# Squared-ReLU attention into a GELU layer: value products copied out of PSUM whole, a first load in two transfers, an identity built on another engine

## The chip, the cores and the metric

The kernel runs on one core of a Trainium2 chip. A core has TensorE (PE; its weight loads are listed apart as PEld), VectorE (DVE), ScalarE (ACT), GpSimd (POOL) and SyncE (SP), each with its own instruction stream, and 16 DMA engines that all queues share. The metric is the device time of one execution in microseconds (us). The time before is 392.25 us, the median of 4 runs (392.04 to 392.69).

## The reference

Attention without softmax over 8 batches, 12 heads, 448 positions and a head size of 64, and then two matrix products with an exact GELU between them:

```python
scores = scale * np.matmul(q, k.transpose(0, 1, 3, 2))      # scale = 1/sqrt(64)
attn = np.maximum(scores, 0.0) ** 2 / S                      # S = 448
attn_out = np.matmul(attn, v)                                # 8, 12, 448, 64
x = attn_out.transpose(0, 2, 1, 3).reshape(B * S, H * D)     # 3584 x 768
h = x @ w_in                                                 # 768 x 2048
g = 0.5 * h * (1.0 + erf(h / sqrt(2)))
return g @ w_out                                             # 2048 x 768
```

All inputs and the output are float32; the kernel computes in bfloat16 with float32 sums.

## The kernel before

The twelve heads of a batch are worked as three *quads* of four heads. For each quad:

- q and k are brought into transposed form, qT and kT. For batches 0 and 1 TensorE transposes them against an identity matrix, `ident` (lines 437 and 465), and DVE or ACT copies the result out of PSUM (lines 308 and 310). From batch 2 on, DVE permutes them into pk and pq (lines 386 and 397) and SP issues DMA transposes (lines 489 and 498).
- TensorE computes scores into a PSUM tile `ps` (line 535), ACT or DVE takes the ReLU with the scale (lines 547 and 549) into `a_sq`, DVE squares it (line 556).
- When the seven blocks of a quad are squared, TensorE forms the value products (`add_av`, line 597) in a PSUM tile `pav` of two banks: 128 partitions x 2 x 448 columns (2 x 224 in batch 0, which is worked in two halves of the positions). Two copies, one for each bank, take them to `xT` in bfloat16 (lines 623 to 630). The planner puts each of the two on DVE or ACT.

The first matrix product (`psh`, line 644) reads a batch's whole xT and w_in, ACT takes the GELU into `h_sb` (line 656); the second (`pso`, line 687) reads h_sb and w_out, DVE copies it to `osb` (line 308) and SP stores it (line 710). The scores and value products of one batch are interleaved with the matrix products of the batch before.

PSUM has eight banks: three tiles of two banks in the pool `w` (ps and pav in turn) and two of one bank in the pool `f` (tp, psh, pso in turn). A tile is given out in turn, so a new ps waits until the tile given out three before it has been read.

The order of instructions on each engine is made when the program is built. The class `Scheduler` keeps, for each operation, its engines with their estimated costs, what it needs and what it frees; the text `ORDER` names the first 270 operations in the order in which they are issued, with the engine of each (P, A, D, G, S), and the rest is placed by the earliest start. So the instructions of all engines stand in one fixed order, and an engine never takes a later one first.

All casting loads go through POOL (lines 257, 274 to 276, 280, 341 and 359). At most eight of them are under way: a ninth is issued when the first has landed. From batch 3 on a load also stands behind `gate` on POOL (line 510), a small copy that reads the transposed q of the batch before, so that loads aren't moved while the transposes are. The k and q of the first quad go in float32 through the queues of ACT and SP instead (lines 771 and 772) and are cast by DVE and ACT: DVE takes the first four of the seven column groups of k (`K_CUT`), ACT q and then the other three. TensorE runs 45 small products of zeros (line 787) until these arrive.

Of the kernel before, what the change touches and what calls it, by code (L numbers as in the profile page):

```python
# [12 lines left out]
B, H, S, D = 8, 12, 448, 64  # L13
# [5 lines left out]
NK = S // KB  # L19
# [16 lines left out]
X_BIAS = -0.2  # L36
# [14 lines left out]
def cols(half):  # L51

    return slice(0, S) if half is None else slice(half * HS, half * HS + HS)
# [3 lines left out]
K_CUT = 4  # L57
# [1 line left out]


ORDER = """
G0 G1 G2 G3 G4 G5 A10 D13 G6 A16 P11 P14 G7 D12 A15 P17 G8 D18 P21 P39 D22 P33 P36 A34 D40
P19 D20 A37 P23 G9 P42 P48 D24 P54 A43 D35 A49 P51 D44 P25 D38 A52 D41 G117 A55 D53 P45 D50
A26 D47 A46 P57 D56 P69 P66 A58 D70 P27 G118 A67 P29 D59 P63 G119 A28 D71 P60 A64 G120 D68
P78 D61 A62 P75 A79 D65 P81 P31 D30 A76 D80 P96 G121 D32 A97 P72 D77 G122 A82 D98 P129 G123
D74 A73 P90 D130 P84 P108 A91 G124 D83 P131 A85 D109 P93 P141 D132 A94 D92 P102 D95 P105
P111 A103 D86 P143 D110 G125 A106 D104 P99 A112 D107 G126 A144 P87 D100 A101 D113 A142 P157
P114 D88 G127 A158 D89 P133 D115 A116 G128 P135 D159 A134 P160 P163 D136 P166 A164 P145 D167
A161 D165 P253 A146 D168 D162 P169 P172 G147 A254 P175 A173 D170 P245 G148 A176 D171 P255
A246 D177 G149 D174 P184 P187 A256 P196 A185 G150 D188 P137 P139 A138 P178 D197 G151 A140  # L70
D186 P193 P211 G152 D180 P247 A212 G153 D213 P249 A248 D179 A194 D198 G154 P263 A250 D195
D229 G155 P223 P220 A264 D189 P190 S235 A224 D221 P265 G156 A191 D225 P267 A266 D192 D222
P199 P217 A268 P214 D231 A218 P257 S236 D215 A200 D219 P259 A258 D216 D201 P181 P208 A260
P205 D230 A209 P261 D182 P251 D183 A262 D210 A206 D233 P202 A252 S237 D207 D232 P226 D234
A203 D204 S238 S239 P269
"""


class Op:
# [1 line left out]

    def __init__(self, engines, fn, deps=(), need=(), frees=(), bias=0.0, mode=None, joint=(),
                 other=0.0):
        self.engines, self.fn, self.deps = engines, fn, list(deps)
        self.need, self.frees, self.bias, self.mode = need, frees, bias, mode
        self.other = other
        self.joint = joint
        self.start = self.done = None  # L90


class Scheduler:
# [47 lines left out]
    def commit(self, est, op, eng, dur, lat):  # L141
        op.start = est
        if eng == "PE":
            self.mode = op.mode
            if est < self.COLD:
                dur, lat = 2 * dur, 2 * lat
        if isinstance(lat, tuple):
            t = max(self.dma, est + dur + 1.0)
            self.dma = t + lat[0] / 390e3
            op.done = self.dma + DMA_LAT  # L150
            self.landed += [op.done] * lat[1]
        else:
            op.done = est + lat
        self.free[eng] = est + dur
        for name in op.need:
            b = self.bufs[name]
            b[b.index(min(b))] = math.inf
        ends = [op.done] + [o.done for o in op.joint]
        if None not in ends:
            for name in op.frees:  # L160
                b = self.bufs[name]
                b[b.index(math.inf)] = max(ends)
        self.log.append((est, op, eng))

    def run(self, fixed):
# [40 lines left out]
def kernel(  # L206
# [9 lines left out]
    nc = tc.nc  # L216
# [24 lines left out]
    k32 = natpool.tile([128, 2, NK * D], F32, tag="pk", name="k32")  # L241
# [9 lines left out]
    def q_view(b, g0, g1, c0, c1):  # L251
        qq = q[b, 4 * g0 : 4 * g1].rearrange("h (p c) d -> p h (c d)", c=NC)
        return qq[:, :, c0 * D : c1 * D]
# [7 lines left out]
    def kv_view(t, b, g0, g1):  # L261

        return t[b, 4 * g0 : 4 * g1].rearrange("h s d -> (h s d)").rearrange(
            "(x p f) -> p x f", p=128, f=NK * D
        )
# [27 lines left out]
    ident = const.tile([128, 128], BF16, tag="ident", name="ident")  # L293
# [10 lines left out]
    V, A = nc.vector, nc.scalar  # L304

    def copy(eng, dst, src):
        if eng == "DVE":
            V.tensor_copy(dst, src)  # L308
        else:
            A.copy(dst, src)  # L310

    def e_copy(n, psum=4):

        d = 0.07 + n / psum / 960
        return ("DVE", d, d + 0.12), ("ACT", 0.12 + 0.00074 * n, 0.24 + 0.00074 * n)

    sch = Scheduler({"w": 3, "a": NA, "f": 2, "osb": 3})
# [10 lines left out]
    QK, SQ, AV, X, GL = {}, {}, {}, {}, {}  # L328
# [193 lines left out]
    def add_steps(todo, bias=0.0, dve=False):  # L522
        for blocks in todo:
# [55 lines left out]
            for blk in blocks:  # L579
                if blk[2] == NK - 1:  # L580
                    add_av(blk, bias)

    def add_av(blk, bias):
        b, g, _, half = blk
        blocks = [(b, g, i, half) for i in range(NK)]
        w = S if half is None else HS
        pav = []

        def fn(e_):
            pav.append(w_pp.tile([128, 2, NB], F32, tag="w", name="pav"))  # L590
            for i, x in enumerate(blocks):
                _, box, o = SQ[x]
                for j in range(2):
                    r = slice(64 * j, 64 * j + 64)
                    for e in range(2):
                        o2 = 64 * (e ^ j)
                        nc.tensor.matmul(  # L597
                            pav[0][o2 : o2 + 64, e, :w],
                            vt[b][r, 2 * g + e, bass.ts(i, D)],
                            box["a2"][r, e, o : o + w],  # L600
                            start=(i == 0),
                            stop=(i == NK - 1),
                        )

        deps = list(dict.fromkeys(SQ[x][0] for x in blocks)) + ld_v[b, g]

        last = {id(SQ[x][1]): x for x in SQ}
        gone = sum(last[id(SQ[x][1])] == x for x in blocks)
        d = 7 * 0.19 * w / S
        op = sch.add(  # L610
            (("PE", d, d + 0.24),), fn, deps, mode="A", bias=bias + AV_BIAS, need=("w",),
            frees=("a",) * gone,
        )
        AV[b, g, half] = op

        def get_x():
            if b not in xT:
                xT[b] = xpool.tile([128, HP, S], BF16, tag="xT", name="xT")
            return xT[b][:, 2 * g : 2 * g + 2, cols(half)]

        old = [o for (bb, *_), o in F1.items() if bb == b - 2]
        xs = X[b, g, half] = []
        for j in range(2):
            xs.append(
                sch.add(
                    e_copy(w, 1), lambda e, j=j: copy(e, get_x()[:, j], pav[0][:, j, :w]),
                    [op] + old, frees=("w",), joint=list(xs), bias=bias + X_BIAS,
                )
            )
        xs[0].joint = [xs[1]]  # L630


    def add_f1(b, m, half=None, bias=0.0):
# [96 lines left out]
    def f2(b):  # L730
        tiles = range(0, 3) if b % 2 == 0 else range(3, 7)
        return [(2.6, add_f2(b // 2, t, n)) for t in tiles for n in range(2)]

    def mix(a, b):

        a, b = list(a), list(b)
        r, n = [], len(a) + len(b)
        na = len(a)
        for i in range(n):
            if a and (not b or (na - len(a) + 1) * n <= (i + 1) * na):  # L740
                r.append(a.pop(0))
            else:
                r.append(b.pop(0))
        return r
# [12 lines left out]
    def slots(first, last):  # L757
# [10 lines left out]
        return out + [[("AV", done)]]  # L768


    nc.scalar.dma_start(k32, kv_view(k, 0, 0, 1))
    nc.sync.dma_start(q32, q_view(0, 0, 1, 0, HC))
    zero = const.tile([128, 128], BF16, tag="zero", name="zero")
    V.memset(zero, 0.0)  # L774
    V.memset(ident, 0.0)
    nc.gpsimd.affine_select(
        out=ident, in_=ident, compare_op=mybir.AluOpType.not_equal, fill=1.0,
        base=0, pattern=[[-1, 128]], channel_multiplier=1,
    )
    warm = const.tile([128, 1], F32, tag="warm", name="warm")  # L780
    V.memset(warm, 0.0)

# [22 lines left out]
    def early(eng, get, src, t):  # L805
        def fn(e):
            get_nat(0)
            copy(e, get(), src)

        n = src.shape[1] * src.shape[2]  # L810
        d = 0.07 + n / 960 if eng == "DVE" else 0.12 + 0.00074 * n
        return sch.add(((eng, d, d + 0.12),), fn, [landed(t)])

    o = early("ACT", lambda: nq[0][:, :4, : HC * D], q32, 5.3)
# [4 lines left out]
    for eng, i0, i1 in (("DVE", 0, K_CUT), ("ACT", K_CUT, NK)):  # L819
        c = slice(i0 * D, i1 * D)  # L820
        o = early(eng, lambda c=c: nk[0][:, :2, c], k32[:, :, c], 5.45)
# [42 lines left out]
    class at_slot:  # L864


        def __init__(self, n):
            self.key = first[n]
# [41 lines left out]
    x1, x2 = f1(B - 1), f2(B - 2)  # L910
    for _, o in x2[:1] + mix(x1, x2[1:]) + f2(B - 1):
        pe_q.append(o)
    sch.run({"PE": pe_q, "POOL": pool_q})
# [1 line left out]
_INS = ['q', 'k', 'v', 'moe_w_in', 'moe_w_out']  # L915
# [26 lines left out]
```

## Time and profile before

| | |
|---|---|
| Median of 4 runs | 392.25 us |
| The profiled execution | 392.41 us |
| Its span in the profile | 390.5 us |
| Granted TensorE clock | full in all 40 slices |
| PE, DVE, ACT, POOL busy | 98%, 49%, 51%, 12% of the span |
| Copies xT<-pav, 448 columns | 22 on DVE, mean 624 ns; 20 on ACT, mean 532 ns |
| Copies xT<-pav, 224 columns | 7 on DVE, mean 385 ns; 5 on ACT, mean 345 ns |
| First k, ACT's queue, 448 KB | 4.6 us from issue to landing |
| First q, SP's queue, 224 KB | 4.4 us from issue to landing |
| Affine select for ident, POOL | 311 ns, at 2.15 us |

A line of the timeline gives start, duration, engine, line of the code, operation, what is written from what, shapes, and in brackets how long the engine had been idle and what released it. PE is busy nearly throughout: its waits are few and have to be looked for one by one. A DMA's "landing" is the time at which those who wait for it may go on.

### The profile page before, as it was taken

To read this page: it belongs to the slowest core of one execution; us is meant where nothing else is said; L and a number is where in the kernel's file an instruction comes from. 1 tells how busy PE (TensorE), PEld (TensorE's weight loads), DVE (VectorE), ACT (ScalarE), POOL (GpSimd) and SP (SyncE) were. 2 spreads that over 40 slices of the span, in tenths; PEclk is the share of its full clock that TensorE was granted. 3 is DMA by queue.
4 is the path that set the end of the run, shared out by engine and by line. 5 is a ranking of instruction groups with operands and counts; after the bars stand their busy time and mean duration, and the time that the engine had idled before them with its cause. 6 is when DMAs were issued, how large, how long until landed. Compare 5 with 4: busy or idle time off the path is not lost.

```text
span 390.5 us, 7973 instructions
## 1 busy us (share of the span) xinstructions
PE 381.5 (98%) x3436; PEld 211.7 (54%) x3437; DVE 189.6 (49%) x350; ACT 200.1 (51%) x304; POOL 45.7 (12%) x69
## 2 busy tenths in 40 slices
PE   8799999998999999999999999999999999999996
PEld 7476554454555555555555555555555555555563
DVE  3999962466636435644555346545355352110121
ACT  4988855753436554565734466366536545222200
POOL 8665304000200200020000200000000000000000
PEclk9999999999999999999999999999999999999999
DMA  9999999999998691689139871370111011100132
GB/s 176 193 203 204 198 176 125 209 202 152 187 179 135 125 177 39 135 126 177 42 68 154 125 131 42 78 146 2 40 27 56 2 42 40 42 14 28 40 81 82
DMA packets 69523, 42.94 MB, mean 110 GB/s; under 512 B 37744, under 2 KB 65904, under 8 KB 69488
## 3 DMA queue, kind: packets, MB, share of 16 engines
q0 software_dynamic: 30512, 22.47, 38.5%
q1 hardware_dynamic: 38672, 19.49, 24.8%
q8 instruction: 27, 0.44, 0.4%
q10 hardware_dynamic: 304, 0.48, 0.3%
q14 instruction: 8, 0.07, 0.0%
HBM read 45.61 MB, written 11.01 MB: 145 GB/s over the span
## 4 chain that ended last, share of the span: by engine, by line
PE 85%; DMA 9%; POOL 2%; DVE 1%; SPq 1%; issue 1%; ACT 0%; POOLq 0%
PE pso L687 36%; PE psh L644 33%; PE ps L535 8%; PE pav L597 7%; DMA nq<-in_q_dram 5%; DMA nk<-in_k_dram 2%; DMA v_sb<-in_v_dram 2%; SPq L498 1%; DMA qT<-pq 1%; POOL nk L341 1%; DVE a_sq L556 0%; POOL nq L257 0%; POOL v_sb L359 0%; DVE osb L308 0%; DVE pq L397 0%
## 5 line engine op out<-in xcount | busy, mean ns | idle before, releaser
L644 PE MATMUL psh<-xT,win_sb 128*128 128x448 bf16 (+1 forms) x804 | 154.3, 345 | 0.1
L687 PE MATMUL pso<-wout_sb,h_sb 128*128 128x384 bf16 (+2 forms) x895 | 151.6, 326 | 0.1
L547 ACT ACTIVATE a_sq<-ps 128x896 bf16<-128x896 f32 (+1 forms) x141 | 123.3, 914 | 48.4 <-PE ps L535 48.2
L556 DVE TENSOR_TENSOR a_sq<-a_sq 128x896 bf16<-128x896 bf16 (+1 forms) x169 | 100.5, 618 | 53.7 <-ACT a_sq L547 53.5
L656 ACT ACTIVATE h_sb<-psh 128x448 bf16<-128x448 f32 x128 | 70.1, 547 | 98.5 <-PE psh L644 98.5
L687 PEld LDWEIGHTS <-h_sb 128*128 128x128 bf16 x896 | 86.2, 98 | 62.5 <-issue 5.8
L644 PEld LDWEIGHTS <-win_sb 128*128 128x128 bf16 x804 | 76.2, 98 | 70.4 <-issue 9.7
L308 DVE COPY osb<-pso 128x384 f32<-128x384 f32 (+2 forms) x56 | 31.2, 557 | 89.6 <-PE pso L687 89.6
L535 PE MATMUL ps<-qT,kT 64*64 64x448 bf16 (+1 forms) x756 | 46.8, 336 | 2.6 <-DVE a_sq L549 0.9
L549 DVE TENSOR_SCALAR a_sq<-ps 128x896 bf16<-128x896 f32 x28 | 30.4, 1090 | 36.0 <-PE ps L535 35.6
L597 PE MATMUL pav<-a_sq,v_sb 64*64 64x448 bf16 (+1 forms) x756 | 37.2, 330 | 0.9 <-ACT a_sq L547 0.4
L535 PEld LDWEIGHTS <-kT 64*64 64x64 bf16 x756 | 18.3, 105 | 24.3 <-issue 19.1
L597 PEld LDWEIGHTS <-v_sb 64*64 64x64 bf16 x756 | 21.3, 107 | 13.6 <-issue 2.7
L308 DVE CAST xT<-pav 128x448 bf16<-128x448 f32 (+1 forms) x29 | 16.3, 566 | 9.3 <-ACT xT L310 4.6
L310 ACT CAST xT<-pav 128x448 bf16<-128x448 f32 (+1 forms) x25 | 12.4, 495 | 15.4 <-PE pav L597 9.7
L510 POOL COPY gate<-qT 128x4 bf16<-128x4 bf16 x5 | 0.9, 188 | 157.3 <-DMA qT<-pq 157.3
L257 POOL DMA_DIRECT2D nq<-in_q_dram x14 | 11.6, 827 | 2.7 <-DMA win_sb<-in_moe_w_in_dram 0.9
L359 POOL DMA_DIRECT2D v_sb<-in_v_dram x14 | 10.6, 755 | 3.1 <-DMA win_sb<-in_moe_w_in_dram 1.9
L341 POOL DMA_DIRECT2D nk<-in_k_dram x13 | 10.0, 767 | 4.7 <-issue 1.5
L397 DVE COPY pq<-nq 112x512 bf16<-112x512 bf16 x36 | 8.2, 287 | 1.5 <-DMA nq<-in_q_dram 1.5
L386 DVE COPY pk<-nk 128x896 bf16<-128x896 bf16 x18 | 6.3, 386 | 1.0 <-DMA nk<-in_k_dram 1.0
L787 PE MATMUL spin<-zero 128*128 128x128 bf16 x45 | 5.0, 314 | 1.0 <-DVE zero L774 1.0
(26 smaller groups left out, 44.2 us busy)
## 6 DMA issues: line engine op xcount, KB each, us to landing
nk<-in_k_dram POOLq DMA_DIRECT2D x5, 672.0 KB, 7.7
nq<-in_q_dram POOLq DMA_DIRECT2D x5, 672.0 KB, 11.4
v_sb<-in_v_dram POOLq DMA_DIRECT2D x5, 672.0 KB, 13.8
out_dram<-osb SPq DMA_DIRECT2D x7, 336.0 KB, 2.8
wout_sb<-in_moe_w_out_dram POOLq DMA_DIRECT2D x2, 1152.0 KB, 11.7
out_dram<-osb SPq DMA_DIRECT2D x8, 288.0 KB, 2.8
v_sb<-in_v_dram POOLq DMA_DIRECT2D x9, 224.0 KB, 8.8
out_dram<-osb SPq DMA_DIRECT2D x8, 240.0 KB, 2.8
```

Of the source, the lines that this page charges most:

```text
L257: nc.gpsimd.dma_start(nq[b][:, 4 * g0 : 4 * g1, c0 * D : c1 * D], q_view(b, g0, g1, c0, c1))
L308: V.tensor_copy(dst, src)
L310: A.copy(dst, src)
L341: nc.gpsimd.dma_start(nk[b][:, 2 * g0 : 2 * g1], kv_view(k, b, g0, g1))
L535: nc.tensor.matmul(ps[64 * j : 64 * j + 64, e, x * w : x * w + w], kT[r, g, i * 128 + 64 * j : i * 128 + 64 * j + 64], qT[r, 2 * g + j, co ...
L547: A.activation(ar, ps, AF.Relu, scale=c_att)
L549: V.tensor_scalar(ar, ps, c_att, 0.0, op0=mybir.AluOpType.mult, op1=mybir.AluOpType.max,)
L556: V.tensor_mul(box["a2"][:, :, :used], ar, ar)
L597: nc.tensor.matmul(pav[0][o2 : o2 + 64, e, :w], vt[b][r, 2 * g + e, bass.ts(i, D)], box["a2"][r, e, o : o + w], start=(i == 0), stop=(i == ...
L644: nc.tensor.matmul(ph[:, x * n : x * n + n], win_sb[:, kd, bass.ts(m + x, 128)], xT[b][:, kd, c], start=(kd == 0), stop=(kd == KD - 1),)
L656: A.activation(hT[b // 2][:, m : m + nm, o + c.start : o + c.stop], box[0][:, :S].rearrange("p (x n) -> p x n", x=nm), AF.Gelu,)
L687: nc.tensor.matmul(po[:, :w], hT[pr][:, kf, bass.ts(t, 128)], wout_sb[:, kf, c], start=(kf == 0), stop=(kf == KF - 1),)
```

## The change

Three things are changed.

1. The value products of a quad leave PSUM in one copy of both banks on one engine, instead of two copies that may go to two engines. The operation's estimated cost is that of the whole size, and the tile is free when it is done, so the field `joint` (free when both are done) goes away.
2. The first k goes in two transfers of ACT's queue, one for each part of `K_CUT`, so that each cast waits for its own part.
3. The identity is an operation of its own on POOL, memset and affine select, at a place that ORDER names (`G1125`): behind the first three loads. Before, DVE cleared it, and POOL's affine select stood between the first load and the second.

ORDER is numbered anew, since there are fewer operations. In the changed program PE has the same instructions in the same order; DVE has 8 xT copies (4 of 2x224 and 4 of 2x448) and ACT 19 (2 of 2x224 and 17 of 2x448); where a merged copy stands between others on these engines differs from before in places.

```diff
-    def __init__(self, engines, fn, deps=(), need=(), frees=(), bias=0.0, mode=None, joint=(),
-                 other=0.0):
+    def __init__(self, engines, fn, deps=(), need=(), frees=(), bias=0.0, mode=None, other=0.0):
...
-        self.joint = joint
...
-        ends = [op.done] + [o.done for o in op.joint]
-        if None not in ends:
-            for name in op.frees:
-                b = self.bufs[name]
-                b[b.index(math.inf)] = max(ends)
+        for name in op.frees:
+            b = self.bufs[name]
+            b[b.index(math.inf)] = op.done
...
-        xs = X[b, g, half] = []
-        for j in range(2):
-            xs.append(
-                sch.add(
-                    e_copy(w, 1), lambda e, j=j: copy(e, get_x()[:, j], pav[0][:, j, :w]),
-                    [op] + old, frees=("w",), joint=list(xs), bias=bias + X_BIAS,
-                )
+
+        X[b, g, half] = [
+            sch.add(
+                e_copy(2 * w, 1), lambda e: copy(e, get_x(), pav[0][:, :, :w]),
+                [op] + old, frees=("w",), bias=bias + X_BIAS,
             )
-        xs[0].joint = [xs[1]]
+        ]
...
-    nc.scalar.dma_start(k32, kv_view(k, 0, 0, 1))
+    for i in (slice(0, K_CUT * D), slice(K_CUT * D, NK * D)):
+        nc.scalar.dma_start(k32[:, :, i], kv_view(k, 0, 0, 1)[:, :, i])
     nc.sync.dma_start(q32, q_view(0, 0, 1, 0, HC))
     zero = const.tile([128, 128], BF16, tag="zero", name="zero")
     V.memset(zero, 0.0)
-    V.memset(ident, 0.0)
-    nc.gpsimd.affine_select(
-        out=ident, in_=ident, compare_op=mybir.AluOpType.not_equal, fill=1.0,
-        base=0, pattern=[[-1, 128]], channel_multiplier=1,
-    )
...
+    def fn_ident(e):
+        nc.gpsimd.memset(ident, 0.0)
+        nc.gpsimd.affine_select(
+            out=ident, in_=ident, compare_op=mybir.AluOpType.not_equal, fill=1.0,
+            base=0, pattern=[[-1, 128]], channel_multiplier=1,
+        )
+
+    sch.add((("POOL", 0.4, 0.5),), fn_ident)
     sch.run({"PE": pe_q, "POOL": pool_q})
```

## The prediction

> **What bounds the kernel now.** I read the page first, for the engines' shares.
>
> ```profile
> PE 381.5 (98%) x3436; PEld 211.7 (54%) x3437; DVE 189.6 (49%) x350; ACT 200.1 (51%) x304; POOL 45.7 (12%) x69
> ```
>
> TensorE is busy 381.5 of 390.5 us, so 9.0 us is all that any change off TensorE can win. Of it 3.6 us is the tail (the last matmul ends at 386.9, then come a copy and the last stores). TensorE's waits are the rest; the trace lists them with total, times and longest:
>
> ```profile
> PE spin L787 <- DVE zero L774: 1.0, 1, 1.0
> PE ps L535 <- DVE a_sq L549: 0.9, 1, 0.9
> PE ps L535 <- ACT a_sq L547: 0.7, 2, 0.4
> PE tp L437 <- DMA nk<-in_k_dram: 0.5, 2, 0.4
> PE ps L535 <- ACT qT L310: 0.5, 1, 0.5
> ```
>
> Cut into windows, all of these but two fall before 20.7 us. TensorE then has no wait until 89, waits at 89.2 (0.15) and 90.7 (0.89), and never again. So the end is set by three things: when TensorE starts its unbroken run at 20.5, how long the stall at 89 to 91 is, and TensorE's own 296 us after it. The chain of waits and the timeline show what ends the two stalls:
>
> ```profile
> 13.35 7.11 DMA nk<-in_k_dram
> 66.51 19.27 DMA nq<-in_q_dram
> ```
> ```profile
> 20.50 0.58 PE L437 MATMUL tp<-ident,nk 128*64 128x128 bf16 x14 [0.19 <-DMA nk<-in_k_dram]
> 85.81 1.30 DVE L397 COPY pq<-nq 112x512 bf16<-112x512 bf16 x6 [1.52 <-DMA nq<-in_q_dram]
> 89.56 1.08 DVE L549 TENSOR_SCALAR a_sq<-ps 128x896 bf16<-128x896 f32 x1
> 90.70 0.38 PE L535 MATMUL ps<-qT,kT 64*64 64x448 bf16 x4 [0.89 <-DVE a_sq L549]
> ```
>
> Both hang on transfers: first keys of batch 1 land at 20.46; queries of batch 3 land at 85.78, VectorE then does six pq copies, an osb copy, three squares, an osb copy and a relu before a score tile comes free. In windows the DMA engines' share is 1.26 to 1.59 from 4 to 57 us at some 200 GB/s: POOL's queue always has a backlog, and a landing comes when the bytes ahead of it are through, not when it was issued.
>
> **Value products.** Before, a quad's two copies run one after the other: the second waits for the first.
>
> ```profile
> 134.83 0.53 ACT L310 CAST xT<-pav 128x448 bf16<-128x448 f32 x1 [0.49 <-PE pav L597]
> ...
> 135.40 0.62 DVE L308 CAST xT<-pav 128x448 bf16<-128x448 f32 x1 [0.27 <-ACT xT L310]
> ```
> ```profile
> 17.00 0.38 DVE L308 CAST xT<-pav 128x224 bf16<-128x224 f32 x1
> 17.41 0.34 ACT L310 CAST xT<-pav 128x224 bf16<-128x224 f32 x1 [0.21 <-DVE xT L308]
> ```
>
> The pair holds its PSUM tile for 135.40+0.62-134.83 = 1.19 us. The forms of after aren't in the trace at their sizes as copies; from 224 and 448 columns ACT goes from 0.345 to 0.532 and VectorE from 0.385 to 0.624, so 896 columns are 0.532+2x0.187 = 0.91 on ACT and 0.624+2x0.239 = 1.10 on VectorE (the relus of 896 f32 columns take 0.92 and 1.09). 54 copies become 27: VectorE 4 half and 4 full, ACT 2 half and 17 full. VectorE's busy time goes from 16.3 to 4x0.62+4x1.10 = 6.9, ACT's from 12.3 to 2x0.53+17x0.91 = 16.5.
>
> [...]
>
> TensorE's order is unchanged, instruction for instruction. *After 24 us* it has no wait but the two above, so shorter holding wins nothing. The loss is that ACT's next relus start 0.38 later (135.26 becomes 135.64). The tightest cover is at 118.63: xT, relu, GELU at 120.18 with 0.20 idle ahead of it, so the GELU slips 0.18, from an end at 120.72 to 120.90; the pso matmuls that need its PSUM slot start at 121.12. Cover left: 0.2. If it were gone, each of the 17 ACT copies would cost TensorE up to 0.38. I cost it at 0.
>
> *From 13 to 20.5 us* ACT is the slow engine. At 13.98 it idles 0.31 for VectorE's half; after, its one copy runs 13.6 to 14.1, so the relus start 0.1 to 0.2 earlier. At 17.41 both the 0.21 idle and the 0.34 copy leave ACT (VectorE does the quad, 17.0 to 17.6), so ACT's next relus move from 17.66 to about 17.0: 0.6 to 0.7 earlier, and the value products at 19.44, which waited 0.42 for one, come some 0.6 earlier. But the next instruction on TensorE is the transpose at 20.50, whose keys land at 20.46: its wait grows from 0.19 to about 0.8, and all is given back. Term: 0 for the end, bounds -0.1 to 0.1 (the landing itself).
>
> *Batch 1's first quad* is where the merged copy hurts. VectorE had put one half into a hole:
>
> ```profile
> 38.93 0.62 DVE L308 CAST xT<-pav 128x448 bf16<-128x448 f32 x1
> 40.26 0.62 DVE L556 TENSOR_TENSOR a_sq<-a_sq 128x896 bf16<-128x896 bf16 x1 [0.70 <-ACT a_sq L547]
> 40.80 0.62 DVE L308 CAST xT<-pav 128x448 bf16<-128x448 f32 x1
> ...
> 51.83 0.39 DVE L386 COPY pk<-nk 128x896 bf16<-128x896 bf16 x1
> ```
>
> After, the whole copy follows the square at 40.26: 40.80 to 41.90 instead of 41.41, so VectorE is 0.48 late. Behind it stand squares, relus and the three pk copies that SP's DMA transposes wait for. Walking VectorE's rows on, the first pk is 0.48 late, the second 0.38, the third (51.83) 0.19, the small holes having taken the rest; the square at 52.29 waits for ACT anyway, so squares and pq copies are on time to 0.03. Value products at 51.94 read the late squares only near 54: hidden. But SP issues the transposes kT at 42.97, 46.5 and 52.24, then four of qT until 61.97; POOL's gate copy waits for them (63.5), and behind the gate stand the loads of wout, nk, nq and v on POOL's queue, nq being the one that lands at 85.78. What reaches the gate is between 0 (the transposes crawl behind POOL's backlog until 57 anyway) and 0.48 (the first pk's lag in full). I take 0.25, near the middle, nearer the last pk's 0.19 that directly precedes the issue at 52.24. TensorE has no wait between, so its stall at 90.7 grows by as much: **+0.25**, bounds 0 and +0.5.
>
> **First k in two transfers.** One issue of 0.47 us more on ACT's queue, ahead of the table load (1.24 to 2.52, then idle to 5.15): hidden by 2.4 us. The packets double from 256 of 1,792 bytes to 512, of 1,024 and 768. What a packet costs follows from the queues' shares of 16 engines in the first 14 us (q10 is ACT's queue with k, q1 SP's with q in 448 packets of 512 bytes):
>
> ```profile
> q10 hardware_dynamic: 272, 0.46, 8.9%
> q1 hardware_dynamic: 464, 0.23, 6.0%
> ```
>
> k's take 1.25 us on each engine, 78 ns for each of 16; q's 0.84, 30 ns for each of 28. A line through the two has 11 ns a packet beside the bytes, so 16 more on each engine cost 0.17 us. VectorE's part could land up to half a microsecond earlier, but TensorE takes q's transposes first, and q's cast on ACT starts at 5.15 and ends 5.77. If q, sharing with smaller packets, lands earlier, TensorE's start can move from 5.90 to 5.70 (end of the spin). ACT's part is cast at 5.67 and not needed before 6.98, so it may land 0.8 late. Term at the start: -0.2 to +0.3, and whatever it is, the keys at 9.4 and 20.46 absorb it. For the end: 0, bounds 0 and +0.17 (if the backlog carries the packets' cost on).
>
> **Identity on POOL.** VectorE loses a memset of 0.11 while idle. On POOL the affine select (0.31) moves from before the second load to behind the third, with a memset (0.10 on one column up to 0.31 like the select): loads two and three issue 0.28 earlier, the later ones 0.1 to 0.35 later. From 4 us the share is over 1.3, so the backlog hides both; ident is done near 4.2 and first read at 5.90. 0, bounds -0.1 and +0.1.
>
> **Sum.** 0 (after 24 us) + 0 (13 to 20.5) + 0.25 (transposes and gate) + 0 + 0 = +0.25. The profiled execution took 392.41 for a span of 390.5, 0.16 over the median of 392.25, so 392.5 as a median. Adding the bounds: -0.2 to +0.87; not all ends meet, so I take 391.9 to 393.0. From no change this measurement tells about 0.2%, 0.8 us (391.5 to 393.0).
>
> **Rivals.**
> *Landings move too (faster).* If POOL's two early loads and a freer VectorE bring the landings at 20.46 and 85.78 forward, TensorE keeps the 0.6 won before 20.5, and the stall of 1.04 at 89 to 91 shrinks by 0.4: 392.25-0.6-0.4 = 391.25. For it: ACT and VectorE are fuller (3.6 to 4.0 us of each 4) than TensorE from 8 to 20. Against: a steady 200 GB/s from 4 to 40. 10%.
> *The late transposes are amplified (slower).* SP issues transposes one behind the other; the third, issued at 52.24, took 2.78 where others take 1.3. If the 0.48 us comes on top there and the split's 0.17 and another 0.35 of queueing add up, the gate is 1.0 late, and the stall takes all of it: 393.25. It decides once the gate is over 0.8 late. For it: nothing on that chain has slack. Against: VectorE's lag has shrunk to 0.19 by then. 20%.
> *Cover gone on ACT (slower).* If every ACT copy delays a GELU past the 0.2 left, 17x0.18 = 3 us: 395.3. Against: one place in three only has a GELU close behind. 5%.
> *The edit does nothing:* VectorE's lag never reaches the gate: 392.2, inside my own range.
>
> **Numbers.** My case 65% (392.5, own range 391.9 to 393.0), the others 10, 20 and 5. The range leaves out the last and the far parts of the first two: 391.5 to 393.3. Faster 0.10, within 0.65, slower 0.25.
>
> **What would show it.** Right: 27 casts xT, 0.91 and 1.09; TensorE waits longer than 0.6 for nk near 20.4; the gate copy near 63.8; the ps wait for VectorE's relu near 91 grown to about 1.1. Wrong: nk for batch 1 landing before 20.2, or a PE wait on h_sb or xT after 100 us.

## The result, and the profile after

The changed kernel takes 393.08 us (median of 49 runs, 391.89 to 395.58), the kernel before 392.54 (74 runs): ratio 1.0021, 95% interval 1.0013 to 1.0029. The interval leaves out 1, so the kernel is slower, by about the 0.2% that the prediction took as the least it can tell from no change; the forecast was 392.5 and no change.

The profiled execution took 392.6 us for a span of 390.8, with TensorE busy for 97% of it. The copies out of PSUM, from the view of one tile's instructions (count, shortest/median/longest in ns, first and last start, forms):

```profile
L305 ACT CAST xT<-pav x19: 540/905/906, 13.5 to 317.9; 128x896 bf16<-128x896 f32 x17, 128x448 bf16<-128x448 f32 x2
L303 DVE CAST xT<-pav x8: 619/854/1092, 16.9 to 332.7; 128x448 bf16<-128x448 f32 x4, 128x896 bf16<-128x896 f32 x4
```

There are 27, at 0.905 on ACT and 1.09 on VectorE: the prices of the prediction (0.91 and 1.10). TensorE's timeline, around 20 and around 90 us:

```profile
18.72 0.86 PE L592 MATMUL pav<-a_sq,v_sb 64*64 64x224 bf16 x28
20.64 0.58 PE L432 MATMUL tp<-ident,nk 128*64 128x128 bf16 x14 [1.05 <-DMA nk<-in_k_dram]
...
89.03 0.38 PE L592 MATMUL pav<-a_sq,v_sb 64*64 64x448 bf16 x4 [0.15 <-DVE a_sq L551]
89.57 0.38 PE L592 MATMUL pav<-a_sq,v_sb 64*64 64x448 bf16 x4 [0.15 <-DVE a_sq L551]
89.76 0.38 PE L530 MATMUL ps<-qT,kT 64*64 64x448 bf16 x4
91.03 0.38 PE L530 MATMUL ps<-qT,kT 64*64 64x448 bf16 x4 [0.89 <-DVE a_sq L544]
```

The value products that started at 19.44 start at 18.72, and the 0.72 is all given back: the wait for batch 1's keys is 1.05 instead of 0.19, and the transposes start at 20.64 instead of 20.50. The stall near 90 has grown in another place than forecast: the wait for the relu stays 0.89, and the squares before it now hold up the value products. The two waits of 0.15 that are listed are one more than before, and the four products ahead of them start 0.49 behind the four before them, where the others are 0.19 apart; the list has no wait there. What is late there was forecast to begin at 40 us; VectorE's timeline:

```profile
40.11 0.63 DVE L551 TENSOR_TENSOR a_sq<-a_sq 128x896 bf16<-128x896 bf16 x1 [1.25 <-ACT a_sq L542]
40.65 1.08 DVE L303 CAST xT<-pav 128x896 bf16<-128x896 f32 x1
...
42.72 0.52 DVE L381 COPY pk<-nk 128x896 bf16<-128x896 bf16 x1
...
86.14 1.30 DVE L392 COPY pq<-nq 112x512 bf16<-112x512 bf16 x6 [1.98 <-DMA nq<-in_q_dram]
```

The whole copy stands behind the square, as the order has it; SP's first transpose is at 43.34 (42.97 before), the gate copy at 63.71 (63.53), the issue of batch 3's queries at 66.99 (66.51), VectorE's copies of them at 86.14 (85.81). TensorE came to 84.5 us 0.14 earlier than before and leaves the stall 0.34 later; from there to the end the two profiles run in parallel. So the end of the chain that the prediction costed at +0.25 is at +0.34. Its links are not all as costed. The second kT transpose is issued at 46.70 (46.52 before), but the third, behind the last pk copy, at 52.20 (52.24 before): beside TensorE, which is 0.14 ahead, 0.10 of the lag is left. The transposes of the queries, after and then before, from SP's timeline:

```profile
54.68 7.46 SPq L493 DMA_TRANSPOSE qT<-pq  x4
```
```profile
55.12 6.86 SPq L498 DMA_TRANSPOSE qT<-pq  x4
```

They start 0.44 earlier and take 0.60 longer, and that is what makes the gate copy late in this execution. From the issue of the third transpose to the gate copy it is 11.51 us here and 11.29 before. Over all 20 profiles of this case it is 11.02 to 12.18 in the eight with the late copy and 11.07 to 12.08 in the twelve without, so it isn't shown that the late copy lengthens it. Nor does the profile show why the median moved by 0.54, and why the runs reach 395.58.

### The profile page after: what moved, and what is told of

The parts are those of the page before. It is cut to its first block, busy times and chain, and to the rows that moved or that the text cites. A ratio compares the mean times of both kernels' runs of the same rounds, so it can differ in the third digit from the quotient of the medians.

```text
span 390.8 us, 7965 instructions
## 1 busy us (share of the span) xinstructions
PE 380.0 (97%) x3436; PEld 210.6 (54%) x3437; DVE 181.1 (46%) x328; ACT 204.0 (52%) x298; POOL 46.0 (12%) x70
## 4 chain that ended last, share of the span: by engine, by line
PE 85%; DMA 9%; POOL 2%; DVE 1%; SPq 1%; issue 1%; ACT 0%; POOLq 0%
PE pso L680 36%; PE psh L637 33%; PE ps L530 8%; PE pav L592 7%; DMA nq<-in_q_dram 5%; DMA nk<-in_k_dram 2%; DMA v_sb<-in_v_dram 1%; SPq L493 1%; DMA qT<-pq 1%; POOL nk L336 1%; DVE a_sq L551 0%; PE tp L432 0%; POOL v_sb L354 0%; DVE osb L303 0%; DVE pq L392 0%
## 5 line engine op out<-in xcount | busy, mean ns | idle before, releaser
L305 ACT CAST xT<-pav 128x896 bf16<-128x896 f32 (+1 forms) x19 | 16.5, 869 | 10.2 <-PE pav L592 10.2
L303 DVE CAST xT<-pav 128x448 bf16<-128x448 f32 (+1 forms) x8 | 6.8, 854 | 5.4 <-PE pav L592 5.3
L432 PE MATMUL tp<-ident,nk 128*64 128x128 bf16 x84 | 3.7, 222 | 1.9 <-DMA nk<-in_k_dram 1.7
```

## The experiments

Ratios are to the kernel before, on the same chip in the same session, with the 95% interval; 0.001 is 0.39 us. Theory A is the chain of the prediction (late copy, transposes, gate, batch 3's queries, stall); Theory B is that the front (k in two transfers, the identity on POOL) costs, which the prediction put at 0.

### The change again, its parts, and the late copy moved

e0_after is the changed kernel. e1_copies has the merged copies alone, e2_front the front alone:

```diff
-    nc.scalar.dma_start(k32, kv_view(k, 0, 0, 1))
+    for i in (slice(0, K_CUT * D), slice(K_CUT * D, NK * D)):
+        nc.scalar.dma_start(k32[:, :, i], kv_view(k, 0, 0, 1)[:, :, i])
...
-G0 G1 G2 G3 G4 G5
+G0 G1 G2 G1152 G3 G4 G5
```

e3_swap is the changed kernel with the copy of batch 1's first quad ahead of the square:

```diff
-A204 G147 D205 P240 A239 D173 A187 D191
+A204 G147 D173 D205 P240 A239 A187 D191
```

> The changed kernel unaltered, as the mark for the others of this series. Theory A (batch 1's late copy reaches the loads of batch 3 through pk, the transposes and the gate): ratio to before 1.001 to 1.002; gate copy 0.2 to 0.4 us later than before's 63.53, TensorE 0.15 us ahead of before between 30 and 88 us and 0.3 to 0.5 behind after 91. Theory B (the two front edits cost it): the same ratio, but already behind at 30 us. In either case executions with a mean granted clock of 0.994 to 0.996, of which the first 50 executions had 11, should be the longest ones, by some 2 us.

> Merged copies alone; first k in one transfer and the identity as before. Theory A: all of the loss, ratio 1.0008 to 1.002, the stall of TensorE near 90 us (1.04 in before) at 1.2 to 1.6 us. Theory B: ratio 1.000, gate copy within 0.1 us of 63.53.

> First k in two transfers and the identity on POOL alone; two copies a quad as before. Theory A: ratio 0.9995 to 1.0005, gate copy within 0.1 us of 63.53. Theory B: 1.001 to 1.002, and more executions with a granted clock under 0.997 than before.

> The changed kernel with one word of ORDER moved: batch 1's first whole copy on VectorE stands ahead of the square that waits for ACT, in the hole from 38.9 to 40.2 us, and not behind it. Theory A: the first pk copy at 42.5 us or earlier instead of 42.72, the loss gone: ratio 0.999 to 1.000, gate copy at 63.5 or before. Theory B, or a loss from ACT's longer copies after 100 us: no change against the changed kernel, ratio 1.001 to 1.002.

Measured: e0_after 1.0024 (1.0008 to 1.0040); e1_copies 1.0007 (0.9991 to 1.0024); e2_front 1.0037 (1.0023 to 1.0052); e3_swap 1.0001 (0.9986 to 1.0017). VectorE in e3_swap:

```profile
38.82 1.09 DVE L291 CAST xT<-pav 128x896 bf16<-128x896 f32 x1
40.15 1.16 DVE L539 TENSOR_TENSOR a_sq<-a_sq 128x896 bf16<-128x896 bf16 x2 [0.24 <-ACT a_sq L530]
...
42.38 0.39 DVE L369 COPY pk<-nk 128x896 bf16<-128x896 bf16 x1
```

The copy fits into the hole, the first pk is 0.34 earlier than after, the gate copy comes at 63.46, the queries' copies at 85.75, and the loss is gone: the mean of its 12 runs is 0.9 us under that of e0_after's 12, with 0.8 either way by their scatter. So the place of this copy costs time, as Theory A has it; the way from the copy to the stall is argued, as said above. But the front alone, which has none of this, loses too: Theory B holds as well. Its 1.0037 is above the 1.0024 of the whole change, and the parts sum to 1.0044, but with these intervals it can't be said that they do not add up.

### Which half of the front

e4_split has only the first lines of e2_front's edit, e5_ident only the identity on POOL.

> Before, with the first k in two transfers and nothing else. The two front edits together gave 1.0037 [1.0023, 1.0052], a gap from the gate copy to the issue of batch 3's queries of 3.28 us where before has 2.98, and a first key of batch 1 some 0.2 later. Theory S (the split does it: more packets, every later transfer late): ratio 1.002 to 1.004, gap unchanged at 2.98, transfers from 10 us on late by 0.2 or more. Theory I (the identity's new place in POOL's instructions does it): ratio 0.999 to 1.001, gap 2.98, stall at 88 to 91 as before, 1.05 in sum.

> Before, with the identity built on POOL behind the third load and nothing else. Theory I: ratio 1.002 to 1.004, the gap from the gate copy to the issue of batch 3's queries 3.28, the stall at 88 to 91 at 1.35 or more in sum. Theory S: ratio 0.999 to 1.001, gap 2.98, stall 1.05.

Measured: e4_split 1.0008 (0.9997 to 1.0018); e5_ident 1.0017 (1.0005 to 1.0028). So the identity's new place costs, and the split alone can't be told from nothing. One price can be read directly, on POOL behind the gate copy. The kernel before, then e4_split, e5_ident and the changed kernel, each from the timeline of POOL:

```profile
63.53 0.19 POOL L510 COPY gate<-qT 128x4 bf16<-128x4 bf16 x1 [19.14 <-DMA qT<-pq]
63.77 1.65 POOL L280 DMA_DIRECT2D wout_sb<-in_moe_w_out_dram  x2
...
66.51 0.95 POOL L257 DMA_DIRECT2D nq<-in_q_dram  x1
```
```profile
64.23 0.19 POOL L510 COPY gate<-qT 128x4 bf16<-128x4 bf16 x1 [20.02 <-DMA qT<-pq]
64.68 1.65 POOL L280 DMA_DIRECT2D wout_sb<-in_moe_w_out_dram  x2 [0.27 <-issue]
...
67.41 0.95 POOL L257 DMA_DIRECT2D nq<-in_q_dram  x1
```
```profile
63.61 0.18 POOL L510 COPY gate<-qT 128x4 bf16<-128x4 bf16 x1 [19.14 <-DMA qT<-pq]
...
66.69 0.95 POOL L257 DMA_DIRECT2D nq<-in_q_dram  x1
```
```profile
63.71 0.18 POOL L505 COPY gate<-qT 128x4 bf16<-128x4 bf16 x1 [19.53 <-DMA qT<-pq]
...
66.99 0.95 POOL L252 DMA_DIRECT2D nq<-in_q_dram  x1
```

From gate copy to queries: 2.98 before, 3.18 with k split, 3.08 with the identity moved, 3.28 with both; e2_front and e0_after have 3.28 too, e1_copies 2.97. It is an idle of "issue", for which the engine waits for nothing that the profile shows, some 60 us behind the two edits. Against the expectations both halves carry a part of it. It holds in all 20 profiles: with k split the first load behind the gate is issued 0.20 later, with the identity moved the queries' load 0.10 later. What makes it is not known. This 0.30 is on the path of Theory A, behind the gate, and the landing carries it on: in 15 of the 16 profiles whose chain of waits has this load, the queries land 18.98 to 19.34 us after their issue (19.27 in before, 19.12 in the first profile of the changed kernel; 19.93 in e7_fill), for issues from 66.30 to 68.11.

The rest of the front's loss (1.0037 is 1.45 us) was not pinned to a place. From 30.3 us on TensorE is 0.30 behind in e2_front and 0.15 in e5_ident, but the three profiles of the changed kernel lie at -0.36, -0.15 and +0.16 there, so one profile can't decide that. And the profiled execution of e2_front was the fastest of its 12 (392.82): TensorE ends 0.57 behind the kernel before in it, so most of the loss isn't in that trace.

### The clock, and the stall made shorter or longer

In the profiles of e0_after and e1_copies TensorE's granted clock falls to half for one stretch of 3.41 us, directly behind the stall. The windows of e0_after, cut at these edges (start and end, length, busy time and count by engine, granted clock, DMA share, GB/s), and those of e4_split around the stretch where it happened there:

```profile
88.57:91.99 3.42, 1.92 (x28) 0.65 (x21) 3.42 (x6) 1.58 (x3) 0.00 (x0) 1.00 1.76 183
91.99:95.40 3.41, 3.41 (x13) 1.57 (x13) 1.79 (x4) 1.17 (x2) 0.00 (x0) 0.50 0.66 131
95.40:98.81 3.41, 3.41 (x22) 1.97 (x20) 0.56 (x1) 0.00 (x0) 0.19 (x1) 1.00 0.75 160
```
```profile
16.05:19.46 3.41, 2.23 (x60) 1.26 (x49) 3.01 (x8) 3.19 (x6) 3.39 (x5) 1.00 1.38 198
19.46:22.88 3.42, 3.42 (x66) 2.71 (x65) 2.62 (x6) 2.35 (x4) 2.63 (x5) 0.50 1.28 203
```

In 91.99 to 95.40 there are 13 products where the next stretch has 22. In e0_after TensorE falls from 0.91 behind the kernel before to 2.59, in e1_copies from 0.34 to 2.02: 1.7 us each, never won back. By estimate from these rows an execution with one such stretch has a mean clock of 1 - 0.5 x 3.41/391 = 0.996 (0.995, 0.995 and 0.996 in the profiles of e0_after, e1_copies and e4_split), so it can be counted without a profile: 0.997 or less in 17 of 74 executions of the changed kernel (11 of 50, 3 of 12, 3 of 12), in 8 of 157 of the kernel before, in 4 of 12 of e1_copies and 3 of 12 of e2_front. In the first 50, the 11 have a mean span of 392.96, the others 391.23. The first explanation was Theory G, that the length of the wait decides; e7_fill and e9_fill2 put work into the stall (the first diff is e7_fill's; e9_fill2 has the block 2, 2, 2 in its place), e8_dose makes it longer:

```diff
+                if blocks[0][:3] == (2, 1, 2):
+                    for _ in range(11):
+                        nc.tensor.matmul(ps[:, 0, :128], zero, zero, start=True, stop=True)
```
```diff
-                permute_q(
+                for _ in range(2 if b == 3 and g < 2 else 1):
+                    permute_q(
```

> After, with 11 products of zeros (128 columns each, about 0.59 us in all) put into the score tile ahead of the scores that precede the stall near 91; the real products overwrite them. They fill part of the stall and take nothing away from what ends it. Theory G (a window of 3.41 us with 1.4 us or more of waiting makes the clock halve for the next window): the waits in a window fall to 0.9 or less, so no execution has a granted clock of 0.997 or lower (after: 14 of 62), the others stay at after's span of 391.2 to 391.5, and the ratio falls from 1.002 to 1.000 to 1.0015. Theory N (the low clocks have nothing to do with the stall): 2 to 4 of 12 stay low, ratio 1.002 to 1.004.

> After, with the 11 products of zeros put directly ahead of the scores before the stall near 91 (in e7_fill they stood one quad earlier, at 78, where there is no stall, and cost 0.75 us of TensorE's time there). Theory G (too little work in one 3.41 us window at 88 to 92 halves the clock for the next one): the wait for VectorE's relu falls from 0.89 to about 0.2 and the end does not move by itself; no or one low clock of 12 (after 14 of 62); mean span of the rest 391.2 to 391.5 as after; ratio 1.000 to 1.0015. Theory N (low clocks come from elsewhere, the first 22 us for instance): 2 to 4 low of 12, ratio 1.002 or more.

> Before, with four of batch 3's six copies of queries on VectorE done twice (the same values again), 4 x 0.217 = 0.87 us ahead of the relu that ends the stall near 91. Nothing else is late. Theory G: the waits near 89 to 92 go from 1.05 to about 1.9 in sum, so that half or more of the executions have a granted clock of 0.994 to 0.996 and a span 1.7 above the rest; the rest is 0.9 above before; ratio 1.004 to 1.007. Theory N: no low clock, as in all 35 executions of before; ratio 1.0015 to 1.003.

Measured: e7_fill 1.0021 (1.0007 to 1.0034), 2 low clocks of 12; its products ran at 78 us, a quad too early, so it tests nothing. e9_fill2 1.0011 (0.9999 to 1.0023), the wait for the relu filled, 2 of 12 low. e8_dose 1.0017 (1.0008 to 1.0025), none of 11. The stall of e8_dose:

```profile
89.23 0.38 PE L598 MATMUL pav<-a_sq,v_sb 64*64 64x448 bf16 x4 [0.44 <-DVE a_sq L557]
...
91.76 0.38 PE L536 MATMUL ps<-qT,kT 64*64 64x448 bf16 x4 [0.90 <-DVE a_sq L550]
```

With two waits of 0.15 between these it waits 1.64 us in all, more than e0_after's 1.49, and its end is 1.1 later than the profile of before, but no clock fell. So the length of the wait alone does not decide, and low clocks come where the stall is filled. The filled stall did not speed the kernel by itself either, as it should not.

### VectorE's order at the stall

The stall exists because VectorE takes its instructions in the order of the program: it stands at the queries' copies until they land near 86 (idle for 1.52 us in the kernel before, 1.98 in the changed one), and then has six copies, squares and a relu to do. e6_cure plans the six copies two score blocks later; e14_acure, e15_bcure and e13_best2 put a third at the old place and the rest directly behind the relu; e17_behind puts all six behind it.

```diff
-            add_pq(b + 1, 0, G, after=at(n))
+            add_pq(b + 1, 0, G, after=at(n + (2 if b == 2 else 0)))
```
```diff
-            add_pq(b + 1, 0, G, after=at(n))
+            if b == 2:
+                add_pq(3, 0, 1, after=at(n))
+                add_pq(3, 1, G, after=[RELU[2, 2, 1, None]], bias=-0.5)
+            else:
+                add_pq(b + 1, 0, G, after=at(n))
```

e6_cure and e14_acure are the changed kernel with the first and the second of these, e15_bcure the kernel before with the second. e18_cswap has merged copies, the old front and e3_swap's exchange; e10_best is e18_cswap with e6_cure's edit, e13_best2 with the second, e17_behind with `add_pq(3, 0, G, ...)` in its place. e11_nk is e10_best with the first keys of batch 1 loaded ahead of the second part of w_in. e16_after is the changed kernel once more.

> After, with VectorE's six copies of batch 3's queries planned two score blocks later, behind the relu on which TensorE waits near 91; no transfer moves but the transposes of these queries, needed at 115 and later. If the later landing of batch 3's queries (86.1 for 85.8) reaches TensorE through this stall alone, and the half clock comes from this stall: the waits at 88 to 92 go from 1.35 to under 0.4, the end comes 1.0 earlier than after's, no low clock, ratio 0.997 to 0.999. If most of after's loss is elsewhere (the first 22 us, or behind 100 us): ratio 0.999 to 1.002 and low clocks as in after.

> The changed kernel with that placing of batch 3's queries on VectorE, all else as it is. If its loss comes through the stall at 88 to 92 (1.35 us of waits, and the half clock behind it): end 1.2 before the changed kernel's and no low clock from there, ratio 0.996 to 0.998, and not more than 0.3 us behind e15_bcure. If a good part comes from the front and goes past the stall: ratio 0.998 to 1.001, 0.6 us or more behind e15_bcure.

> The kernel before with the same placing of batch 3's queries. Its stall of 1.05 us goes: ratio 0.997 to 0.998. If the merged copies are worth 0.3 us once nothing behind them waits, e13_best2 is 0.2 to 0.5 us faster than this one; if they are worth nothing, the two are equal to 0.15.

> The changed kernel unaltered. Ratio 1.001 to 1.004 as twice before. If the low clocks belong to its stall: 2 to 4 of 12 with 0.996 or less, where e14_acure has none or one; if they belong to the first 22 us, e14_acure has as many.

> Merged copies, the old front, and VectorE's copy of batch 1's first quad ahead of the square it stood behind. By the term of the prediction that puts +0.25 on that copy's place: 0.2 to 0.4 less than e1_copies (1.0007), ratio 0.999 to 1.0005, gate copy at 63.5, stall of 1.05 in sum. If the merged copies cost in another place: ratio 1.001 or more.

> The merged copies with the old front, VectorE's copy of batch 1's first quad moved ahead of the square it stood behind (as e3_swap), and the queries' copies of batch 3 two blocks later (as e6_cure). If the merged copies by themselves win the 0.3 us that e1_copies shows between 30 and 84, and the stall goes: end 1.0 to 1.3 before that of before, ratio 0.9965 to 0.9985. If the merged copies cost as such (by clocks or ACT's queue): ratio above 0.999.

> e10_best with the first keys of batch 1 loaded ahead of the second part of w_in instead of behind it. The prediction said that TensorE's 0.6 won before 20.5 by the merged copies is given back because these keys land at 20.46. If so: they land at 18.5 or earlier, the wait of 0.9 to 1.05 before the transposes at 20.5 goes, and with the later stall gone too the end comes 0.6 to 1.0 before e10_best's, ratio 0.994 to 0.997. Rival: the second part of w_in lands 1 to 2 later and TensorE waits for it (or for the queries of batch 1) instead, so the end is e10_best's to 0.2.

> e10_best with the queries' copies of batch 3 placed finer on VectorE: a third at once at 85.8, two thirds directly behind the relu near 88.8. In e10_best the transposed queries came 1.27 us late at 98; here VectorE ends its copies at 89.8 instead of 91.0, so they come 0.1 to 0.3 late or in time, and no wait stays between 21 and 380. Expected: 0.9 to 1.2 us less than e10_best, ratio 0.994 to 0.9955. Rival: the transposes are held by what else moves on the DMA queues, and the wait at 98 stays above 0.8: ratio as e10_best's.

> e10_best with all six copies of batch 3's queries directly behind the relu near 88.8 instead of two squares later. VectorE waits for no landing ahead of the relu, so the wait at 91 stays away as in e10_best; the copies end at 90.0 instead of 91.0, so the wait for the transposed queries at 98 falls from 1.27 to 0.2 to 0.4: 0.8 to 1.1 less than e10_best, ratio 0.994 to 0.9955. Rival: the transposes' time is set by the queues, the wait at 98 stays near 1.2, ratio 0.9965 to 0.9975.

| | ratio | 95% | low clocks |
|---|---|---|---|
| e6_cure (after, copies later) | 1.0005 | 0.9989 to 1.0021 | 4 of 12 |
| e14_acure (after, finer) | 0.9996 | 0.9984 to 1.0008 | 1 of 12 |
| e16_after (after, unaltered) | 1.0006 | 0.9995 to 1.0018 | 3 of 12 |
| e15_bcure (before, finer) | 0.9989 | 0.9972 to 1.0005 | 2 of 12 |
| e18_cswap (merged, old front, exchange) | 0.9994 | 0.9981 to 1.0008 | 0 of 12 |
| e10_best (e18_cswap, copies later) | 0.9969 | 0.9955 to 0.9982 | 0 of 12 |
| e11_nk (e10_best, keys earlier) | 0.9965 | 0.9954 to 0.9976 | 1 of 12 |
| e13_best2 (e18_cswap, finer) | 0.9969 | 0.9956 to 0.9982 | 0 of 7 |
| e17_behind (e18_cswap, all behind the relu) | 0.9972 | 0.9956 to 0.9988 | 1 of 11 |

What follows, in the order of what is well shown. Merged copies with the old front and VectorE's order mended in two places take 391.5 us (e10_best) where the kernel before takes 392.36: a version faster than both. What the placing alone is worth is seen in e17_behind and e18_cswap, which differ in nothing else and ran together: 0.6 us in the mean, with 0.5 either way. With the same finer order, the one with the changed front and without the exchange (e14_acure) is 0.0027 or 1.06 us behind the one with the old front and the exchange (e13_best2). This is the price of the front and the late copy together. It was not taken at an equal stall: both profiles have the wait of 0.9 for the relu, but in e14_acure TensorE also waits 0.3 for an osb copy and 0.2 for a square there, and the queries are issued at 68.11 instead of 67.07. The expectation for e14_acure asked what the loss is without the stall; the finer order did not remove it, and e6_cure put a wait of 1.29 at 98 in its place, so that question was not answered.

Whether merged copies win by themselves is open: e13_best2 is 0.8 us ahead of e15_bcure, but the intervals overlap. They don't lose: e18_cswap 0.9994. Beside e1_copies' 1.0007 that is a second pair for the place of the late copy, 0.5 us as expected, but from two chips and with intervals that overlap.

Several expectations were missed: e13_best2 and e17_behind were to reach 0.9955 or less, e15_bcure 0.998 or less. And e16_after, the changed kernel once more, was to be at 1.001 or more; its 1.0006 can't be told from the kernel before.

The stall could be moved, not removed. The waits of TensorE behind 21 us, in e10_best, e17_behind and e13_best2 (total, times, longest):

```profile
PE ps L532 <- DMA qT<-pq: 1.3, 1, 1.3
```
```profile
PE ps L533 <- DMA qT<-pq: 1.0, 1, 1.0
```
```profile
PE ps L533 <- DVE a_sq L547: 0.9, 1, 0.9
```

With the copies behind the relu, batch 3's scores at 98 wait for the transposed queries; a us earlier on VectorE (e17_behind against e10_best) is worth 0.3 there. With a third of them at the old place (e13_best2), VectorE again stands until they land at 86.37, and the old wait is back.

e11_nk bears on the give-back at 20.5. Its transposes start at 19.36, 1.14 earlier than before, and TensorE then waits 0.8 at the scores at 21 and longer for batch 1's queries; from 30.3 us on it is at -0.04. The rival was right: behind each landing stands the next one.

## Why the prediction was wrong, step by step

*The copies, and 13 to 20.5 us.* Right in mechanism, and near in size: 27 copies at 0.905 and 1.09, 0.72 won ahead of 20.5 (0.6 forecast), and given back to the keys (wait 1.05 for 0.19, about 0.8 forecast).

*After 24 us, 0.* Right: TensorE has no wait behind 92 us in the profile, nowhere for xT or h_sb.

*Batch 1's first quad, +0.25.* That this copy's place costs is shown, on one chip, by the exchange: e3_swap, which cures only this, is at 1.0001 beside e0_after's 1.0024 (e16_after, on another chip, is at 1.0006). The path is not shown. The last pk copy, forecast 0.19 late, was at 51.79 (51.83 before), and the gate came late by longer transposes behind it. That the gate was near 63.8 (63.71) is in part luck: it is 63.07 to 64.20 in the three profiles of the changed kernel. The growth of the stall was forecast at the relu and came at the value products ahead of it.

*First k in two and identity on POOL, 0 each.* This is the step that failed. "From 4 us the share is over 1.3, so the backlog hides both" is an argument about bandwidth in the first 20 us; the front alone measures 1.0037 (1.4 us), the identity 1.0017, the split 1.0008 and not clear of 1. Beside merged copies the front's price is less sure: e0_after and e1_copies differ by 0.0017, with intervals that overlap. The part that was found is not where the prediction looked: 0.20 and 0.10 us more between the gate copy and the issue of batch 3's queries, 60 us later, on the one chain that has no slack. There the premise "a landing comes when the bytes ahead of it are through, not when it was issued" fails: the queries land 19.0 to 19.3 us after their issue, early or late. The rest, about 1 us in e2_front, has no place yet, and its cause stays open.

*A term that was missing.* The sum was made from one execution at full clock. By their mean clock, TensorE runs one stretch at half clock in 17 of 74 executions of the changed kernel; where the profiles show it behind the stall it costs 1.7 us. In the first 50 executions the mean time is 0.82 us above that of the kernel before, and 0.43 without the 11 low clocks, so this term is about half of the loss if the kernel before had none there (it had 8 in the 157 executions counted above). On e0_after's chip the mean span is 391.97 against 390.87 for the kernel before, and without the low clocks 391.50: 0.63 of the 1.10 us is the chain and the front, 0.47 the clock. Either alone is under the 0.8 us that the prediction took as the least it can tell; together they reach it. The division isn't the same everywhere: in e16_after the three low ones were not longer than the others (391.1 against 391.0). What makes the clock fall in one execution and not in the next is not settled.

*Chances.* The rival "the late transposes are amplified" was the case on the right side, at 393.25; its mechanism, a gate more than 0.8 late, did not happen (0.18 in the first profile, 0.67 in e0_after), so that its number was near is luck.

## What to carry to other kernels

An edit at the head of a program isn't free because the queue is full there (the front alone measured 1.0037 here): ask which chain without slack runs through the same engine's instruction stream later, and price its issue gaps too (0.20 and 0.10 us here). An engine whose order is fixed and tightly packed should not stand at a landing with work behind it on which TensorE waits (VectorE stood 1.98 us at the queries here, and TensorE waited 0.89 for its relu); move the copy behind that work, and then look for the next date that it must meet (here 98 us). And a forecast of a few tenths of a per cent from one profile needs the spread of the granted clock beside it (0.997 or less in 17 of 74 executions of the changed kernel here).

## What the runs showed of the hardware

In the traces the granted clock fell whole stretches of 3.41 us behind the start of its record at full: 25 in e0_after (6.65 to 91.99) and 4 in e4_split (5.81 to 19.46), and in the first profile of the changed kernel, with the last product done, 113 (3.75 to 389.45). Where a fall came amid the work, the clock was at half for one stretch and then full again, as the rows of e0_after show (0.50 from 91.99 to 95.40). In the profile of before the record at full starts at 6.36. TensorE was not idle ahead of the falls: it was busy for 1.92 of 3.42 us in e0_after and for 2.23 of 3.41 in e4_split. Its busy time in a window doesn't decide by itself; e14_acure has the same 1.92 in one of its early windows, and the clock stayed:

```profile
13.13:16.54 3.41, 1.92 (x60) 1.45 (x63) 3.34 (x6) 3.23 (x7) 1.44 (x2) 1.00 1.50 190
```

One estimate from the traces does separate them, made afterwards and not tested: the time that a window's products need for their columns alone (products of 384 columns start 0.163 us apart in the profile of before, taken here for each column alike; four products on quarters of the array counted once). As shares it is 0.32, 0.41 and 0.38 of the window ahead of the three falls seen in 20 profiles, and 0.44 or more in every other window up to 340 us (the lowest are 0.44 in before, from 16.60 on, and 0.46 in the first profile of the changed kernel, from 10.58 on). It stays a guess, for e8_dose speaks against it: in the rows of its stall a window that starts between about 88.1 and 89.4 would be under 0.44 by the same estimate, which would be two executions of five if the windows start anywhere with equal chance, and none of its 11 had a low clock.
